# Tail token tiles stored in two halves, and the bias rows of three chunks computed four units sooner, in an attention, layer-norm and feed-forward kernel

## The chip, the cores and the metric

The kernel runs on one core of a Trainium2 chip. The metric is the device time of one launch in microseconds (us). TensorE is called PE in the rows, VectorE DVE, ScalarE ACT, GpSimd POOL, and SyncE SP; SP computes nothing here and issues most of the DMAs, so its rows are those of a queue (SPq).

## What is computed

Attention with a position bias made by a small network, over 4 batches, 8 heads, 576 positions and 64 channels, and behind it a layer norm and a feed-forward block of 512 to 2048 to 512 channels. All inputs are float32.

```python
scores = scale * np.matmul(q, k.transpose(0, 1, 3, 2))
x = (psi_rel / psi_i)[..., None]
h = np.maximum(x @ w1 + b1, 0.0)
bias = h @ w2
scores = scores + bias.transpose(2, 0, 1)[None, :, :, :]
...
xn = (x - mu) / np.sqrt(var + 1e-06) * g_ln
ch = np.maximum(xn @ w_ch1, 0.0) @ w_ch2
return (x + ch).astype(np.float32)
```

The bias depends on the two positions and the head, not on the batch.

## The kernel before

**Units.** The 576 query rows are four chunks of 128 rows (c = 0 to 3) and a tail of 64 rows (c = 4). A unit u is one batch, one chunk and one head (a tail unit holds two heads); there are 144, in the order of the list `ORD`. For a unit, PE forms the scores (`qk`, L391, tile sps), DVE adds the bias and takes the row minimum (`softmax1`, L434), ACT takes the exponential (L438) and a float16 copy (L443, tile e), DVE the float16 rest (L462, L464), SP issues a DMA transpose of that pair (L470, into pt, or into wend for every fifth unit), and PE multiplies with V (`pv`, L480, tile xps). The e tiles are four buffers, and one comes free when its transpose has landed.

**Token tiles.** When the eight heads of 128 tokens are there, the layer norm follows (`ln1`, `ln2`), its result goes through a DMA transpose too (L601, xT), and the feed-forward block runs in steps: 48 matmuls of 128 columns (`ffn_w1`, L709, tile hps, one buffer), the two halves of its ReLU on ACT (L714) and on DVE (L717), and 12 matmuls of 512 columns (`ffn_w2`, L736, tile y). DVE adds y to the tile (L747), and after the last step SP stores it (L751). The 64 tail tokens of two batches share one tile, which is stored by L753. There are 18 tiles, two of them tail tiles.

**Bias rows.** The bias is made in 36 groups of 16 query rows, eight for a chunk. A group is four ReLU instructions (`bias_relu`, one on DVE at L162 and three on ACT at L160), four float32 matmuls, each 32 columns wide, into four quarters of one PSUM tile (`bias_mm`, L181, tile bps; each is two passes, so a whole group reads x8 in the trace and one matmul x2), two ACT copies into a tile ev (L187), and a write of ev to a table in DRAM (L211, nb<-ev). Units read the table back with L326 (ldb<-nb, 128 rows of one head); these reads wait for the chunk's last write. The tiles r, ev, t and u are seven buffers of one pool. Line 922 sets in which unit a group is begun: the eight groups of chunks 1 to 3 are spread over 24 units that end ten units ahead of the chunk's first unit, one group every third unit.

**Order.** The Python code sets the order in which work is offered, and a scheduler that comes with the language merges it into one fixed instruction list for each engine. Each engine goes through its list in order and waits on semaphores.

Of the kernel before, what the change touches and what calls it, by code (L numbers as in the profile page):

```python
# [22 lines left out]
def kernel(  # L23
# [13 lines left out]
    V, S, G, T, SY = nc.vector, nc.scalar, nc.gpsimd, nc.tensor, nc.sync  # L37
# [100 lines left out]
    def after(ins, dep):  # L138
        if dep is not None:
            tc.add_manual_dep(ins.ins, dep.ins.name,  # L140
                              mybir.DependencyInfo(mybir.DependencyClass.Sync,
                                                   mybir.DependencyReason.DATA),
                              reason="pace")
# [73 lines left out]
    for n, (b, c) in enumerate(ORD):  # L217
# [6 lines left out]
    cfirst = {c: min(u for (_, cc), u in ustart.items() if cc == c) for c in range(5)}  # L224
    gorder = [g for c in corder for g in range(8 * c, min(36, 8 * c + 8))]
    gend = {c: sum(len(range(8 * x, min(36, 8 * x + 8))) for x in corder[:corder.index(c) + 1])
            for c in range(5)}
# [178 lines left out]
    def spin(n, last=None):  # L406
        ps = ps_h.tile([128, 512], F32, tag="h", name="spin")
        ones = one_sb.bitcast(BF16)
        for _ in range(n):
            m = T.matmul(out=ps[:, 0:256], lhsT=ones[:, 0:128], rhs=ones, start=True, stop=True)  # L410
            if last is None:
                tc.keep_in_program_order(m)
            else:
                tc.add_manual_dep(m.ins, last.ins.name,
                                  mybir.DependencyInfo(mybir.DependencyClass.NoSync,
                                                       mybir.DependencyReason.DATA),
                                  reason="order")
            last = m
# [3 lines left out]
    def softmax1(u):  # L422
        if not 0 <= u < NU:
            return
        b, c, h = units[u]
        ps = st.pop(u)
        t = ep.tile([128, EW], F32, tag="e", name="t")[:, 0:SEQ]
        m = small.tile([128, 1], F32, tag="m", name="m")
        key = (seg[vis[u]], c, h)
        bias = bt[key]  # L430
        buse[key] -= 1
        if not buse[key]:
            bfree[0] += 1
        ttri[u] = V.tensor_tensor_reduce(out=halves(t), in0=ps[:, :, 0:HS], in1=halves(bias), scale=-0.125,  # L434
                               scalar=3e38, op0=ALU.add, op1=ALU.min, accum_out=m)
        if h == 0:
            l8[b, c] = small.tile([128, NH], F32, tag="l8", name="l8")
        S.activation(t, t, AF.Exp, bias=m, scale=-1.0, accum_out=l8[b, c][:, h:h + 1])  # L438
        if nat_pv(b, c):
            et[u] = (t, None)  # L440
            return
        e16 = e16p.tile([128, 1152], F16, tag="e16", name="e16")
        S.activation(e16[:, 0:SEQ], t, AF.Copy, scale=E_SCALE)  # L443
        et[u] = (t, e16)
# [297 lines left out]
    def ffn_y():  # L742
        while yq:
            k, g, t, y, last = yq.pop(0)
            b, c = tiles[blocks[k][t]]
            x = xt[b, c].rearrange("p a d -> p (a d)")
            V.scalar_tensor_tensor(out=x, in0=y, scalar=ycs[:, g:g + 1], in1=x,  # L747
                                   op0=ALU.mult, op1=ALU.add)
            if last:
                if c < 4:  # L750
                    SY.dma_start(out=out[b, c * 128:c * 128 + 128, :], in_=x)  # L751
                else:
                    SY.dma_start(out=out[b:b + 2, 512:576, :], in_=x)  # L753

    jobs = [(k, qq) for k in range(NBL) for qq in range(4)]
    cur_job = []
# [103 lines left out]
    u = 0  # L860
    while u < NU + 6 or jobs or cur_job or pend or yq:
        if u >= NEARLY:
            ffn_y()
        if u in FILL:
            with tc.high_priority(offset=-600):
                spin(FILL[u], lastpv[0])
        softmax1(u)
        if u == 0:
            for ins in gate:
                after(ins, ttri[0])  # L870
            gate.clear()
            gate_on[0] = False
        ustep[0] = u
        issue_loads(u)
        softmax2(u - 1)
        flush()
        for _ in range(2):
            if wload:
                load_w()
        for _ in range(8):  # L880
            if wdec and 32 - len(wdec) < 2 + (4 * max(0, u - 1) + 2) // 3:
                f, i = wdec.pop(0)
                decode_w(f, i)
                if i == 1 and f + 1 == GROUPS[GOF[f]][1]:
                    w_scale(GOF[f])
        while mm_done[0] < ngroup:
            bias_mm(gorder[mm_done[0]])
            mm_done[0] += 1
        if u % 2:
            first = qk(u + 1)  # L890
            if u >= 27 and first is not None:
                after(first, ttri[max(ttri)])
            qk(u + 2)
        while npv <= u - (LAG if u < 38 else LAG + 1):
            if pv(npv):
                lnq.append([u, len(avail_at) + len(lnq)])
            npv += 1
        for fn in todo.pop(u, []):
            fn()
        for qq in range(4):  # L900
            if wdone[0] >= 8 * qq + 8 and qq not in wready_at:
                wready_at[qq] = u
        if u < NU + 9:
            nav = len([a for a in avail_at if a <= u])
            goal = sum(2 * NF * len(bl) // 4 for bl in blocks if bl[-1] < nav)
            nxt = min((steps_av[bl[-1]] for bl in blocks if bl[-1] >= nav), default=NU + 9)
            mbank += max(0.0, (goal - (ntot - nmicro) - mbank)) / max(1, nxt - u)
            mbank = min(mbank, 2.0)
        else:
            mbank = 1.0  # L910
        flush_lo()
        ffn_y()
        while mbank >= 1.0:
            if not ffn_micro(u):
                break
            mbank -= 1.0
            nmicro -= 1
            if mbank >= 1.0:
                ffn_y()
        bneed = NP + 1 + u if u < 8 else 12  # L920
        for c in (1, 2, 3):
            bneed = max(bneed, gend[c] - 8 + min(8, (u - cfirst[c] + 34) * 8 // 24))
        if u < 28:
            bneed = min(bneed, 12)
        if ngroup < min(36, bneed):
            bias_relu(gorder[ngroup], 1 if u >= 24 else 2)
            ngroup += 1
        for _ in range(2):
            if wspl:
                split_w(*wspl.pop(0))  # L930
        for it in list(lnq):
            if it[0] == u - 1:
                ln1(it[1])
            if it[0] == u - 2:
                ln2(it[1])
                avail_at.append(u + (3 if u < NEARLY else 2))
                lnq.remove(it)
        u += 1
# [53 lines left out]
```

## Time and profile before

| | |
|---|---|
| time, median of 3 runs | 680.51 us (680.23 to 681.94) |
| the profiled execution: time, span | 679.99 us, 678.2 us |
| PE busy | 647.7 us, 96% of the span |
| DVE, ACT, POOL busy | 457.8, 392.0, 97.4 us |
| granted TensorE clock, mean | 0.985 of full speed |

Busy time is the time in which an engine's instructions run. A row of a timeline gives start, duration, engine, line, operation, and in square brackets the idle time before it and what ended that.

### The profile page before, as it was taken

The page shows a single profiled execution, that of the slowest core. Times are in us where ns is not written, and L with a number is a line of the kernel's source. Part 1 is how long each engine was busy: PE and PEld are TensorE (multiplying, and loading weights), DVE is VectorE, ACT ScalarE, POOL GpSimd, SP SyncE. Part 2 cuts the span into 40 slices and gives each one's busy share as a digit, 9 for nine tenths or more (in the row PEclk, how much of TensorE's full clock was granted, in tenths as well). Part 3 has the DMA queues.
Part 4 walks back from the last instruction along what each step waited for, and adds up shares of the span by engine and source line. Part 5 has one row for each costly group of instructions (what it writes and reads, how often), then busy time and mean ns, then how long its engine had stood idle before and what let it go on. Part 6 is the DMA issues. An engine that isn't in the chain of part 4 may idle for free.

```text
span 678.2 us, 19142 instructions
## 1 busy us (share of the span) xinstructions
PE 647.7 (96%) x7929; PEld 448.4 (66%) x7929; DVE 457.8 (68%) x1061; ACT 392.0 (58%) x777; POOL 97.4 (14%) x163
## 2 busy tenths in 40 slices
PE   6889996998999889999899999999999999999997
PEld 4447774676466666666667766666776677677775
DVE  6588999778757567686766575757576676766322
ACT  5565847478957447787764577576554455444110
POOL 5312321011000011111101110111011120000000
PEclk9989997899999999999899999999999999999999
DMA  8999885444659996868869789789996976744100
GB/s 312 294 404 331 307 294 161 143 91 115 143 122 148 223 246 156 173 156 164 172 149 239 134 183 181 136 197 181 201 200 144 166 153 125 121 98 87 33 16 17
DMA packets 186955, 117.24 MB, mean 173 GB/s; under 512 B 163956, under 2 KB 164084, under 8 KB 186868
## 3 DMA queue, kind: packets, MB, share of 16 engines
q1 hardware_dynamic: 177124, 81.00, 55.8%
q0 software_dynamic: 9600, 34.84, 16.6%
q8 instruction: 62, 1.02, 0.6%
q10 hardware_dynamic: 144, 0.18, 0.1%
q14 instruction: 25, 0.20, 0.1%
HBM read 60.51 MB, written 15.63 MB: 112 GB/s over the span
## 4 chain that ended last, share of the span: by engine, by line
PE 50%; DVE 0%; ACT 0%; issue 0%
PE hps L709 19%; PE y L736 18%; PE sps L391 6%; PE xps L480 6%; PE bps L181 1%; DVE v L369 0%; DVE x L747 0%; DVE e L462 0%; ACT e L443 0%; DVE x L516 0%; ACT t L438 0%; DVE e L464 0%
## 5 line engine op out<-in xcount | busy, mean ns | idle before, releaser
L709 PE MATMUL hps<-xT,w 128*128 128x128 f16 x3240 | 196.4, 220 | 5.8 <-DVE hh L717 2.6
L709 PEld LDWEIGHTS <-w 128*128 128x128 f16 x3240 | 184.6, 98 | 11.5 <-issue 5.2
L736 PE MATMUL y<-w,hh 128*128 128x512 f16 x810 | 189.1, 381 | 1.9 <-ACT hh L714 1.8
L438 ACT ACTIVATE t<-t,m 128x576 f32<-128x576 f32 x144 | 111.0, 771 | 132.8 <-DVE m L434 132.2
L736 PEld LDWEIGHTS <-hh 128*128 128x128 f16 x864 | 79.7, 98 | 90.6 <-ACT hh L714 3.3
L462 DVE SCALAR_TENSOR_TENSOR e<-t,e 128x512 f16<-128x512 f32 x120 | 82.8, 690 | 81.8 <-ACT e L443 81.5
L434 DVE CUSTOM_DVE_ANT_0 t<-sps,ldb 128x576 f32<-128x576 f32 x144 | 105.9, 753 | 31.4 <-PE sps L391 21.2
L391 PE MATMUL sps<-kf,qf 64*128 64x288 f32 (+1 forms) x640 | 96.6, 436 | 3.5 <-DVE m L434 3.5
L443 ACT ACTIVATE e<-t 128x576 f16<-128x576 f32 x120 | 80.8, 679 | 9.8 <-DMA pt<-e 3.5
L714 ACT ACTIVATE hh<-hps 128x512 f16<-128x512 f32 x72 | 42.0, 583 | 53.4 <-PE hps L709 47.9
L717 DVE SCALAR_TENSOR_TENSOR hh<-hps,hh 128x512 f16<-128x512 f32 x72 | 49.4, 687 | 34.0 <-ACT hh L714 33.5
L391 PEld LDWEIGHTS sps<-kf,qf 64*128 64x128 f32 (+1 forms) x640 | 48.2, 176 | 35.6 <-issue 17.5
L480 PEld LDWEIGHTS <-pt 128*128 128x128 f16 (+1 forms) x1456 | 49.3, 100 | 30.5 <-issue 24.9
L747 DVE SCALAR_TENSOR_TENSOR x<-y,ycs,x 128x512 f32<-128x512 f32 x58 | 43.4, 748 | 32.2 <-PE y L736 32.0
L480 PE MATMUL xps<-v,pt 128*128 128x64 f16 (+1 forms) x1456 | 59.0, 195 | 1.9 <-DMA pt<-e 1.1
L291 POOL DMA_DIRECT2D kf<-in_k_s_dram x56 | 31.1, 556 | 161.4 <-PE sps L391 114.3
L304 POOL DMA_DIRECT2D qf<-in_q_main_dram x32 | 18.5, 577 | 162.4 <-PE xps L480 82.6
L187 ACT ACTIVATE ev<-bps,cb_sb,par_sb 128x144 f32<-128x144 f32 (+27 forms) x48 | 26.0, 593 | 26.2 <-PE bps L181 26.0
L160 ACT ACTIVATE r<-psi_sb,par_sb 128x448 f32<-128x448 f32 (+23 forms) x72 | 39.7, 614 | 0.0
L569 POOL TENSOR_SCALAR rs<-mv 128x1 f32<-128x1 f32 x18 | 9.9, 549 | 146.3 <-DVE mv L568 138.3
L438 ACT ACTIVATION_READ_ACCUMULATOR t<-t,m 128x1 f32 x144 | 27.0, 188 | 0.0
L181 PE MATMUL bps<-r,nw_sb 128*32 128x448 f32 (+24 forms) x200 | 26.9, 494 | 0.0
(121 smaller groups left out, 641.4 us busy)
## 6 DMA issues: line engine op xcount, KB each, us to landing
kf<-in_k_s_dram POOLq DMA_DIRECT2D x56, 288.0 KB, 4.8
w<-in_w_ch_dram SPq DMA_DIRECT2D x22, 512.0 KB, 8.7
ldb<-nb SPq DMA_DIRECT2D x32, 288.0 KB, 4.5
qf<-in_q_main_dram POOLq DMA_DIRECT2D x32, 256.0 KB, 4.6
nb<-ev SPq DMA_DIRECT2D x24, 296.0 KB, 3.4
vf<-in_v_p_dram POOLq DMA_DIRECT2D x16, 320.0 KB, 7.5
out_dram<-x SPq DMA_DIRECT2D x18, 256.0 KB, 2.1
wend<-in_w_ch_dram SPq DMA_DIRECT2D x8, 512.0 KB, 4.8
```

What stands on the lines that cost most here:

```text
L160: S.activation(r[:, 0:n], psi_sb[:, 0:n], AF.Relu, bias=pr_sb[:, g4:g4 + 1], scale=1.0)
L391: m = T.matmul(out=o, lhsT=l, rhs=kk, start=True, stop=True, tile_position=(64 * hf, 64 * e))
L434: ttri[u] = V.tensor_tensor_reduce(out=halves(t), in0=ps[:, :, 0:HS], in1=halves(bias), scale=-0.125, scalar=3e38, op0=ALU.add, op1=ALU.mi ...
L438: S.activation(t, t, AF.Exp, bias=m, scale=-1.0, accum_out=l8[b, c][:, h:h + 1])
L443: S.activation(e16[:, 0:SEQ], t, AF.Copy, scale=E_SCALE)
L462: V.scalar_tensor_tensor(out=e16[:, 640:1152], in0=t[:, 0:512], scalar=E_SCALE, in1=e16[:, 0:512], op0=ALU.mult, op1=ALU.subtract)
L480: T.matmul(out=o, lhsT=p[:, m], rhs=v[:, j, a, :], start=(i == 0), stop=(i == len(ops) - 1))
L709: T.matmul(out=h[:, idx * n:idx * n + n], lhsT=w[:, wo + kk * 128:wo + kk * 128 + 128], rhs=xT[k][:, xo + kk, 0:n], start=(i == 0), stop=( ...
L714: S.activation(hh[:, 0], h, AF.Relu)
L717: V.scalar_tensor_tensor(out=hh[:, 1], in0=h, scalar=0.0, in1=hh[:, 0], op0=ALU.max, op1=ALU.subtract)
L736: T.matmul(out=yps[k][t], lhsT=hh[:, a, o:o + 128], rhs=w[:, wo:wo + 512], start=(f == f0 and i == 0), stop=(f == f1 - 1 and i == 2))
L747: V.scalar_tensor_tensor(out=x, in0=y, scalar=ycs[:, g:g + 1], in1=x, op0=ALU.mult, op1=ALU.add)
```

## The change

Two edits. The store of a tail tile, one DMA with a 2 x 64 x 512 pattern in DRAM, becomes two DMAs of 64 x 512 each. And the number 34 in the rule that begins the groups becomes 38, so that each group of chunks 2 and 3 is begun four units sooner. For chunk 1 other limits in the same rule bind (nothing of it before unit 28, one group a unit): only its last two groups move, from units 35 and 38 to 34 and 35.

```diff
-                    SY.dma_start(out=out[b:b + 2, 512:576, :], in_=x)
+                    for e in range(2):
+                        SY.dma_start(out=out[b + e, 512:576, :], in_=x[64 * e:64 * e + 64])
...
         for c in (1, 2, 3):
-            bneed = max(bneed, gend[c] - 8 + min(8, (u - cfirst[c] + 34) * 8 // 24))
+            bneed = max(bneed, gend[c] - 8 + min(8, (u - cfirst[c] + 38) * 8 // 24))
```

The first edit changes no other row in any engine's list. The second reorders PE, DVE, ACT and SP from the 352-column group of chunk 1 on. POOL's list stays as it is.

PE, the last two groups of chunk 1 (352 and 336 columns). Before, the four matmuls of a group stand together, the first group behind a step of the feed-forward block:

```order
L709 LDWEIGHTS wend
L709 MATMUL hps<-xT,wend 128x128
L181 MATMUL bps<-r,nw_sb 32x352 x4
L480 LDWEIGHTS pt
L480 MATMUL xps<-v,pt 128x64
```

and the second ahead of a pair of tail scores:

```order
L736 MATMUL y_2974<-wend,hh 128x512
L181 MATMUL bps<-r,nw_sb 32x336 x4
L391 MATMUL sps<-kf,qf 64x288 x8
L480 LDWEIGHTS wend
L480 MATMUL xps<-v,wend 128x64
```

With the change the first group is four single matmuls; one stands seven feed-forward matmuls ahead of this piece, and the other three are these:

```order
L181 MATMUL bps<-r,nw_sb 32x352
L391 MATMUL sps<-kf,qf 128x288 x4
L181 MATMUL bps<-r,nw_sb 32x352
L709 LDWEIGHTS wend
L709 MATMUL hps<-xT,wend 128x128
L181 MATMUL bps<-r,nw_sb 32x352
```

The second group, a feed-forward step sooner than before, is in three pieces among matmuls of the V product; the third, a single matmul too, stands three V matmuls behind this piece:

```order
L480 MATMUL xps<-v,pt 128x64
L181 MATMUL bps<-r,nw_sb 32x336 x2
L480 LDWEIGHTS pt
L480 MATMUL xps<-v,pt 128x64
L181 MATMUL bps<-r,nw_sb 32x336
L480 LDWEIGHTS pt
L480 MATMUL xps<-v,pt 128x64
```

Each of the sixteen later groups stands in PE's list with its four matmuls together, before and with the change.

SP, around the store of the first tail tile. Before (numbers behind e_ and x_ tell tiles apart):

```order
L211 DMA nb_125<-ev 16x8x592
L470 DMA_TRANSPOSE pt<-e_2822 128x9x128
L753 DMA out_dram<-x 2x64x512
L601 DMA_TRANSPOSE xT<-x_2872 128x8x128
L470 DMA_TRANSPOSE pt<-e_2880 128x9x128
L470 DMA_TRANSPOSE pt<-e_2965 128x9x128
L470 DMA_TRANSPOSE pt<-e_3001 128x9x128
L751 DMA out_dram<-x 128x512
L211 DMA nb_125<-ev 16x8x592
L326 DMA ldb<-nb_125 128x576 x3
L470 DMA_TRANSPOSE wend<-e_3098 128x9x128
```

and with the change, from the same write on:

```order
L211 DMA nb_125<-ev 16x8x592
L754 DMA out_dram<-x 64x512 x2
L211 DMA nb_125<-ev 16x8x592
L470 DMA_TRANSPOSE pt<-e_2839 128x9x128
L601 DMA_TRANSPOSE xT<-x_2889 128x8x128
L470 DMA_TRANSPOSE pt<-e_2898 128x9x128
L326 DMA ldb<-nb_125 128x576 x5
L751 DMA out_dram<-x 128x512
L470 DMA_TRANSPOSE pt<-e_2983 128x9x128
L470 DMA_TRANSPOSE pt<-e_3011 128x9x128
```

The chunk's last write of bias rows has moved ahead of five DMAs, four of them transposes, and five table reads follow three transposes later instead of three right behind the write.

PE, near the second tail store, at the step of the feed-forward block that uses weights w_129 to w_132. Before, its 48 L709 matmuls are followed by one unit's scores, nine V matmuls (the last is shown) and a bias group, and then at once by the first of its own L736 matmuls:

```order
L480 LDWEIGHTS pt
L480 MATMUL xps<-v,pt 128x64
L181 MATMUL bps<-r,nw_sb 32x369 x4
L736 LDWEIGHTS hh
L736 MATMUL y_5215<-w_129,hh 128x512
```

With the change the 48 matmuls of the next step (w_133 to w_136) stand ahead of them:

```order
L709 LDWEIGHTS w_136
L709 MATMUL hps<-xT,w_136 128x128
L736 LDWEIGHTS hh
L736 MATMUL y_5234<-w_129,hh 128x512
L736 LDWEIGHTS hh
```

A whole L709 step now lies between the matmuls that fill hps and those that read the hh made from it.

## Rows read from the trace of the kernel before

**Rows 1.** The page, its head and part 1: span, busy time (share of span).

```profile
span 678.2 us, 19142 instructions
PE 647.7 (96%) x7929; PEld 448.4 (66%) x7929; DVE 457.8 (68%) x1061; ACT 392.0 (58%) x777; POOL 97.4 (14%) x163
```

**Rows 2.** Busy time by stretch: stretch, its length, engines, granted clock, DMA share, GB/s.

```profile
200.00:260.00 60.00, 56.46 (x821) 38.91 (x819) 38.38 (x92) 34.69 (x71) 6.81 (x12) 1.00 0.97 190
...
326.00:340.00 14.00, 12.00 (x171) 9.72 (x170) 11.47 (x23) 9.81 (x18) 2.11 (x3) 0.88 0.86 174
340.00:672.00 332.00, 332.00 (x4228) 234.34 (x4227) 201.29 (x458) 165.47 (x324) 35.02 (x57) 1.00 0.69 140
```

**Rows 3.** Waits of PE, 200 to 260 us: total us, times, longest.

```profile
PE hps L709 <- DVE hh L717: 2.6, 2, 1.3
PE xps L480 <- DMA wend<-e: 0.5, 1, 0.5
PE xps L480 <- DVE x L543: 0.4, 1, 0.4
```

**Rows 4.** DMA, 208 to 220 us: 40 slices, busy tenths and GB/s; one issue's landing.

```profile
DMA  8899999939617538994999866111111199999997
GB/s 111 213 367 236 266 258 213 175 27 75 61 55 178 185 142 236 251 142 105 94 82 51 53 22 42 55 48 48 48 48 55 38 181 281 288 191 293 432 493 307
...
xT<-x SPq DMA_TRANSPOSE x1, 9.6
```

**Rows 5.** DMA, 327 to 338 us: GB/s in 40 slices.

```profile
GB/s 402 321 177 144 243 195 40 128 286 211 30 0 30 37 52 45 45 52 54 97 128 179 228 227 342 201 197 143 74 74 48 48 48 52 55 271 284 283 217 263
```

**Rows 6.** The sixteen ordinary stores of 128 rows (L751): issue to landing.

```profile
DMA to landing us min/median/max: 2.0/2.1/4.8
```

**Rows 7.** DMA issues, 193 to 198 us: count, KB each, median us to landing.

```profile
ldb<-nb SPq DMA_DIRECT2D x2, 144.0 KB, 3.3
pt<-e SPq DMA_TRANSPOSE x1, 3.2
```

**Rows 8.** Timeline of SP's queue: start, us to issue, line.

```profile
207.06 1.31 SPq L470 DMA_TRANSPOSE pt<-e  x1
208.46 0.83 SPq L753 DMA_DIRECT2D out_dram<-x  x1
209.39 5.07 SPq L601 DMA_TRANSPOSE xT<-x  x1
...
223.53 0.58 SPq L211 DMA_DIRECT2D nb<-ev  x1
228.76 1.28 SPq L326 DMA_DIRECT2D ldb<-nb  x3
```

**Rows 9.** Timeline of ACT and PE, 223 to 225.5 us.

```profile
223.21 0.68 ACT L443 ACTIVATE e<-t 128x576 f16<-128x576 f32 x1 [2.71 <-DMA pt<-e]
...
223.80 0.58 ACT L714 ACTIVATE hh<-hps 128x512 f16<-128x512 f32 x1
...
225.41 2.84 PE L709 MATMUL hps<-xT,w 128*128 128x128 f16 x48 [1.28 <-DVE hh L717]
```

**Rows 10.** Timeline of PE, 196 to 204.5 us: bias matmuls and what follows them.

```profile
196.47 0.81 PE L181 MATMUL bps<-r,nw_sb 128*32 128x368 f32 x2
197.21 1.25 PE L736 MATMUL y<-w,hh 128*128 128x512 f16 x5
...
203.60 0.80 PE L181 MATMUL bps<-r,nw_sb 128*32 128x352 f32 x8
204.33 0.58 PE L480 MATMUL xps<-v,pt 128*128 128x64 f16 x14
```

**Rows 11.** Timeline of DVE, ACT and PE, 329 to 334 us.

```profile
329.41 0.76 DVE L434 CUSTOM_DVE_ANT_0 t<-sps,ldb 128x576 f32<-128x576 f32 x1 [1.29 <-DMA nb<-ev]
...
332.48 0.58 ACT L714 ACTIVATE hh<-hps 128x512 f16<-128x512 f32 x1
...
333.11 0.61 PE L736 MATMUL y<-w,hh 128*128 128x512 f16 x2 [1.57 <-ACT hh L714]
```

## The prediction

> **What bounds the kernel now.** First the page's busy times: PE is busy for 647.7 of 678.2 us, and no other engine for more than 68% [rows 1]. A share over the whole span says little, so next comes the busy time by stretch. From 340 to 672 us PE is busy in every microsecond at full clock [rows 2]: nothing that the change takes from another engine or from DMA can shorten that stretch, and a change there can only hurt. What can be won lies where PE stands still behind the first moved instruction, at about 201 us: 60 - 56.46 = 3.54 us between 200 and 260, and 14 - 12.00 = 2.00 us between 326 and 340 [rows 2]. In the second stretch the granted clock also averages 0.88, that is, part of it ran at the lower level, 1.2 GHz, directly after PE had stood; (1 - 0.88) x 14 = 1.7 us. So 7.2 us is the most that can come back. Then the list of PE's waits says what ended those gaps: of the 3.5 us, 2.6 are two waits for hh (1.3 each), 0.5 a transpose, 0.4 a DVE result [rows 3]. In the second stretch 1.57 us are again a wait for hh [rows 11].
>
> **The tail store.** Before, it is one DMA issued at 208.46 [rows 8]. In the DMA view of that stretch the strip falls to one tenth and 38 to 55 GB/s for seven slices of 0.3 us in a row, and the same 48 GB/s returns behind the second tail store [rows 4, 5]. One tenth of 16 engines is about two. 256 KB at 48 GB/s take 5.5 us, where the ordinary stores of the same size land in a median of 2.1 us, issue and all [rows 6]. I read it as a DMA that runs on two engines, one for each value of its outer dimension. What makes this matter stands behind it in SP's list: the transpose xT takes 5.07 us to issue, where the transpose ahead of the store took 1.31, and 9.6 us to land [rows 8, 4]. The others follow late. Their e buffers come free late, so ACT, which works in order, stands 2.71 us ahead of an L443 at 223.21 and only then reaches the L714 that PE needs; L717 follows, and PE has stood for 1.28 us [rows 9].
>
> Do two stores of 64 x 512 each use all engines? The trace has no such store. The nearest rows are the two loads of 64 rows, 144 KB each, which land in 3.3 us [rows 7]; at two engines' 48 GB/s each alone would need 3.1 us and the pair 6. Ordinary stores give 2.1. I take the ordinary behaviour. Two issues instead of one cost SP at least nothing and at most another 0.83 us [rows 8]; the in-order queue behind them has just won about 4 us (5.07 less 1.31), so they cost nothing.
>
> The Trainium skill, DMA: Bandwidth & Descriptors, Why a DMA increments its semaphore by 16 and not by 1, states how many engines a DMA takes: the largest number up to 16 that divides the slowest dimension of both sides, so 2 for the old store and 16 for either new one. The trace agrees on the old one with its 48 GB/s; no run so far shows the new one.
>
> Term: the wait at 225.41 goes, **-1.28 us**. Bounds: 0 (if the transposes are late for another reason too) and -1.28.
>
> **The split groups.** The part that costs stands in PE's list. The last two groups of chunk 1 were four matmuls together and become four single ones, and a pair with two singles. In the trace the 352-column group together holds PE from 203.60 to 204.33, 0.73 us. A single matmul of the 368-column group holds it from 196.47 to 197.21, 0.74 us [rows 10]. So the four quarters run side by side, and one quarter alone costs as much as all four; a pair must then cost that much too. Then the first group costs 4 x 0.73 instead of 0.73, and the second 3 x 0.73 instead of 0.73: 5 x 0.73 = **+3.6 us** of PE. Nothing hides it where PE is the bound. It would be hidden only as far as PE would have stood anyway soon behind it: bounds 0 and +3.6. I take it whole, since I count those waits as gone.
>
> A rule of the skill would make it dearer still: TensorEngine Tiling (Array Packing), Key Properties, says that changing the tiling mode drains TensorE, and each single matmul adds two such changes. The trace shows no price for it, 0.74 us for a single matmul against 0.73 for a group; by the row the sum stays at +3.6, by the rule it would be larger by an amount that the page doesn't give.
>
> **The rest of the first stretch.** Behind the wait at 225.41, PE stands 2.26 us more by 260 (1.3 + 0.5 + 0.4). In SP's list the chunk's last row write goes out at 223.53, and the table reads behind it at 228.76 [rows 8]; transposes stand behind those. With the change that write comes ahead of four transposes, and five reads stand together behind three of them. The write's new place is directly behind the store, which goes out at 208.46 now; with the store's 0.83 us and the split's 3.6 us it goes out near 213, ten us earlier, so the reads find it landed, and the later transposes no longer share the DMA engines with as many of them. Against that, the first group of chunk 2 now falls into the same 250 us. I take half: **-1.1 us**, bounds 0 and -2.26.
>
> **The second stretch.** At 329.41 DVE's L434 has waited 1.29 us for a write of bias rows to release a buffer of the common pool; ACT's L714 slips to 332.48, and PE waits 1.57 us with its L736 [rows 11]. PE could not fill the time, since before the change that L736 comes almost directly behind the L709 matmuls it depends on. Two things move it: groups begun four units sooner put another group's write there, and in the new list a whole L709 step lies between. That step is 2.84 us long [rows 9], more than the 1.57 us of the wait. So the 2.00 us and the 1.7 us of clock go: **-3.7 us**, bounds 0 and -3.7.
>
> **What costs nothing.** The sixteen other moved groups keep their four matmuls together; their ACT, DVE and DMA work is the same and lies beside a PE that is busy in all of 340 to 672 us [rows 2]. Their writes pass transposes in SP's list by one or two places each, 0.6 us of issue [rows 8]. If that cover goes, a late transpose stops PE for about what the known waits were, 0.4 to 1.3 us.
>
> **Sum.** -1.28 + 3.6 - 1.1 - 3.7 = -2.5 us against the profiled execution's 679.99: 677.5. That execution lies 0.5 us under the median of the three runs, 680.51, so against the median it is **678.0 us**, 0.37% less. With all waits gone it is 3.6 less, 676.9; nothing in the trace allows more, apart from the spread of the runs.
>
> **Rivals.**
> *The gain is eaten.* The store does what it should, but one new wait appears. The nearest candidate is SP's row write of the 336-column group, which now stands ahead of a transpose and waits for ACT's L187, which waits for the last single matmul, up to 3.6 us later than without the split. PE, ACT and DVE behind that transpose then stand. The price lies between the known waits, 0.4 us [rows 3] and 2.71 us [rows 9], say 1 to 2: 679.0 to 680.0, within 0.3% of before. For it: SP's list is in order, and DMA is 0.97 busy there [rows 2]. Against: the transposes are no longer held up by the store, which took more from them than the split does.
> *Slower: the writes of bias rows are the cause, not the store.* Only the wait at 225.41 goes, and the other two remain, because a row write holds a pool buffer or SP's list wherever it is put. Then -1.28 + 3.6 = +2.3 us, 682.8. It decides as soon as less than 1.6 us of the 7.2 comes back. For it: the wait at 329.41 names the write, not the store. Against: PE's new order covers that place.
> *The halves use few engines as well.* Then the store does as before, -1.28 falls away, and the rest stands: 679.3. Against: the 64-row loads.
> *The cost of the split is hidden.* If the waits of the first stretch are set by DMA alone and stay where they are in time, the 3.6 us fall into them and nothing is lost or won there; only the second stretch is won: 680.5 - 3.7 = 676.8.
>
> **Chances.** 0.3% is 2.0 us, about what a measurement of this kernel can tell from no change; with the split's 3.6 us, 5.6 of the 7.2 us must come back for faster, and the forecast has 6.1, near that border. The forecast with its neighbours (5.6 us and more, 0.44; split hidden, 0.08) 0.52; eaten 0.24 and few engines 0.10, together 0.34; slower 0.14. So faster 0.52, same 0.34, slower 0.14. The likeliest case alone spans 676.9 to 678.5. The range for 8 in 10 goes from 676.4, under that floor by the 0.5 us by which executions differ, up into the slower case, to 681.8.
>
> **What would show it.** Right: no stretch of one-tenth DMA behind the tail stores, the xT transpose behind the first issued in about 1.3 us, no wait for hh near 225; seven separate holds of 0.7 us for the two groups; PE without a gap, at full clock, from 320 to 340. Wrong: 48 GB/s still there; single matmuls that cost less than 0.7 us each; PE busy time up by 3.6 us with gaps that stay; a clock below 1.00 anywhere behind 200 us.

## The result, and the profile after

| | before | changed |
|---|---|---|
| median of 6 runs each, us | 680.66 (679.91 to 685.05) | 689.02 (687.20 to 693.01) |
| ratio, 95% interval | | 1.0111 (1.0085 to 1.0138) |
| profiled execution: time, span, us | 679.99, 678.2 | 693.01, 691.2 |
| granted TensorE clock, mean | 0.985 | 0.978 |

The changed kernel is 8.4 us slower. The forecast was 678.0 us, and the range ended at 681.8. The profiled execution is the longest of the six, so sizes are taken from the medians and places from the trace. In the experiments below, eight executions that lie over 1.5% above the fastest of their kernel, four of them above 1000 us, are left out of medians and ratios. Head and part 1 of the page of after (columns as in [rows 1]):

```profile
span 691.2 us, 19138 instructions
PE 654.9 (95%) x7929; PEld 452.5 (65%) x7929; DVE 457.6 (66%) x1061; ACT 390.8 (57%) x777; POOL 95.4 (14%) x163
```

PE is busy 7.2 us longer than in [rows 1] with the same 7929 matmuls; DVE and ACT do what they did. The busy time by stretch of after (stretch, length, engines, clock, DMA share, GB/s) tells where the rest is:

```profile
200.00:260.00 60.00, 55.60 (x675) 35.87 (x675) 33.55 (x80) 32.22 (x66) 5.13 (x9) 0.94 0.86 177
260.00:340.00 80.00, 78.48 (x1076) 54.74 (x1071) 54.65 (x132) 58.58 (x122) 10.39 (x19) 1.00 0.80 163
340.00:400.00 60.00, 56.88 (x704) 39.49 (x704) 40.53 (x93) 34.14 (x68) 5.80 (x10) 0.97 0.86 168
...
326.00:340.00 14.00, 14.00 (x196) 10.14 (x193) 8.58 (x24) 10.21 (x21) 1.60 (x3) 1.00 0.86 164
```

In the stretch from 326 to 340 us, where PE stood for 2.00 us at a clock of 0.88 [rows 2], PE is busy throughout and at full clock. But from 200 to 260 PE now stands 4.4 us, with the clock at 0.94; it stands 1.5 us between 260 and 340, and 3.1 us between 340 and 400, at 0.97, where it never stood before [rows 2]. Standing and half clock (the latter (1 - 0.94) x 60 + (1 - 0.97) x 60 = 5.4 us) are 14.4 us here, against 5.5 + 1.7 = 7.2 us behind 200 us before. Add 3.5 us for the split (below): 10.7 of the 13.0 us by which the spans differ. The first bias matmul starts at 156.0 us instead of 153.3, after a part in which the lists are the same: that is variation between executions, and covers the rest.

PE's waits in after, 200 to 400 us (total us, times, longest):

```profile
PE hps L709 <- DVE hh L717: 6.3, 3, 3.1
PE xps L480 <- DMA pt<-e: 2.7, 2, 2.4
```

The wait for hh of [rows 3] is still the first, longer and later. The longest one, in the timeline of after, 345 to 362 us:

```profile
345.10 1.49 SPq L754 DMA_DIRECT2D out_dram<-x  x2
...
346.69 0.56 SPq L211 DMA_DIRECT2D nb<-ev  x1
...
347.87 0.22 DVE L464 SCALAR_TENSOR_TENSOR e<-t,e 128x64 f16<-128x64 f32 x1
...
349.19 0.22 DVE L464 SCALAR_TENSOR_TENSOR e<-t,e 128x64 f16<-128x64 f32 x1
...
351.52 0.35 SPq L326 DMA_DIRECT2D ldb<-nb  x1
...
351.99 4.83 SPq L470 DMA_TRANSPOSE pt<-e  x2
...
359.30 0.68 ACT L443 ACTIVATE e<-t 128x576 f16<-128x576 f32 x1 [4.05 <-DMA pt<-e]
...
359.88 0.58 ACT L714 ACTIVATE hh<-hps 128x512 f16<-128x512 f32 x1
...
360.75 0.68 DVE L717 SCALAR_TENSOR_TENSOR hh<-hps,hh 128x512 f16<-128x512 f32 x1
...
361.49 0.80 PE L709 MATMUL hps<-xT,w 128*128 128x128 f16 x6 [3.12 <-DVE hh L717]
```

Read it from the bottom. PE waits 3.12 us for hh; hh is late because ACT's L714 stands behind an L443 that waited 4.05 us for an e buffer; the buffer is held by a transpose that SP issued only at 351.99. Above it stands the reason: the chunk's last row write was issued at 346.69, the first table read of chunk 2 directly behind it, and that read has to wait until the write has landed. The DMA view of 344 to 360 us has the write's landing, 4.8 us after its issue, that is at 351.5:

```profile
nb<-ev SPq DMA_DIRECT2D x1, 296.0 KB, 4.8
```

SP goes through its list in order, so from 347.25 to 351.52 it issues nothing, although the two e tiles for the next transposes had been finished at 348.1 and 349.4 (the two L464). The list of the queue's own waits gives 4.2 us to this read, ended by the DMA nb<-ev. The Trainium skill, Perfetto Trace Analysis, Per-instruction lifecycle: what the profiler-reported window actually captures, says that an instruction's wait for a semaphore lies outside the time recorded for it. The trace agrees: the read has 0.35 us, and in the timeline the 4.3 us are only to be seen as a hole between two rows. No transpose is issued from 345.0 to 352.0, 7 us.

SP's list of before holds the same write and read; here is its timeline, 336 to 362 us:

```profile
346.86 1.87 SPq L470 DMA_TRANSPOSE wend<-e  x1
348.89 1.29 SPq L470 DMA_TRANSPOSE pt<-e  x1
350.69 0.53 SPq L211 DMA_DIRECT2D nb<-ev  x1
353.73 1.29 SPq L326 DMA_DIRECT2D ldb<-nb  x3
355.19 3.57 SPq L470 DMA_TRANSPOSE pt<-e  x2
```

There the read waited 2.5 us, two transposes had just gone out, and 5.0 us passed without one: PE did not wait. With the change the write stands directly behind the two halves of the tail store, and ahead of transposes that are ready. It is the place that counts, not the length of the wait: over its whole span the queue of before waits 10.5 us for row writes ahead of table reads, in four waits of up to 4.6 us, and that of after 6.7 us, in two of up to 4.2.

The other place, SP's queue in after, 204 to 250 us:

```profile
213.25 1.16 SPq L754 DMA_DIRECT2D out_dram<-x  x2
216.26 0.55 SPq L211 DMA_DIRECT2D nb<-ev  x1
...
218.44 1.78 SPq L601 DMA_TRANSPOSE xT<-x  x1
...
221.91 2.87 SPq L326 DMA_DIRECT2D ldb<-nb  x5
224.87 0.43 SPq L751 DMA_DIRECT2D out_dram<-x  x1
225.48 7.21 SPq L470 DMA_TRANSPOSE pt<-e  x2
...
234.65 9.37 SPq L470 DMA_TRANSPOSE pt<-e  x3
```

and ACT and PE there (timeline of 232 to 243 us):

```profile
240.46 0.58 PE L480 MATMUL xps<-v,pt 128*128 128x64 f16 x14 [2.38 <-DMA pt<-e]
240.50 0.68 ACT L443 ACTIVATE e<-t 128x576 f16<-128x576 f32 x1 [5.24 <-DMA pt<-e]
...
242.70 0.58 PE L709 MATMUL hps<-xT,w 128*128 128x128 f16 x4 [1.65 <-DVE hh L717]
```

The reads find their write landed, as the prediction said. But five of them, 288 KB each, go out together, the transposes behind them take 7.21 us for two and 9.37 us for three to issue, and PE stands 2.38 and then 1.65 us. From 220 to 246 us the transposes into pt and wend take a median of 8.3 us from issue to landing, the longest 11.7; in before these are 5.5 and 6.7.

The DMA view of after, 212 to 226 us (count, KB each, median us to landing), for the store:

```profile
out_dram<-x SPq DMA_DIRECT2D x2, 128.0 KB, 2.3
...
xT<-x SPq DMA_TRANSPOSE x1, 5.1
```

The halves land in 2.3 us, near the ordinary stores' 2.1 [rows 6], and the xT behind them in 5.1 us instead of 9.6 [rows 4]. The second pair of halves, at 345.10, takes 5.0 us to land. And PE's list, 204 to 215 us, for the split:

```profile
204.37 0.78 PE L181 MATMUL bps<-r,nw_sb 128*32 128x352 f32 x2
205.09 0.56 PE L709 MATMUL hps<-xT,wend 128*128 128x128 f16 x7
...
212.66 0.76 PE L181 MATMUL bps<-r,nw_sb 128*32 128x336 f32 x4
213.35 0.20 PE L480 MATMUL xps<-v,pt 128*128 128x64 f16 x1
```

A single matmul holds PE for 0.72 us, a pair for 0.69; the seven pieces hold it for 4.9 us where two groups held it for 1.4, so the split costs 3.5 us.

### The profile page after: what moved, and what is told of

Its sections match the earlier page's. It is cut to its first block, busy times and chain, and to the rows that moved or that the text cites. A ratio compares the mean times of both kernels' runs of the same rounds, so it can differ in the third digit from the quotient of the medians.

```text
span 691.2 us, 19138 instructions
## 1 busy us (share of the span) xinstructions
PE 654.9 (95%) x7929; PEld 452.5 (65%) x7929; DVE 457.6 (66%) x1061; ACT 390.8 (57%) x777; POOL 95.4 (14%) x163
## 4 chain that ended last, share of the span: by engine, by line
PE 46%; DMA 2%; ACT 2%; DVE 1%; issue 0%; SPq 0%; DVEq 0%; ACTq 0%
PE hps L709 17%; PE y L736 17%; PE sps L391 6%; PE xps L480 5%; DMA nb<-ev 1%; PE bps L181 1%; DMA pt<-e 1%; ACT e L443 0%; ACT v L366 0%; ACT t L438 0%; ACT ev L187 0%; DVE e L462 0%; ACT r L160 0%; DVE v L369 0%; DVE t L434 0%
## 5 line engine op out<-in xcount | busy, mean ns | idle before, releaser
L709 PE MATMUL hps<-xT,w 128*128 128x128 f16 x3240 | 199.8, 222 | 9.5 <-DVE hh L717 6.3
L709 PEld LDWEIGHTS <-w 128*128 128x128 f16 x3240 | 187.7, 99 | 15.7 <-issue 9.5
L736 PE MATMUL y<-w,hh 128*128 128x512 f16 x810 | 189.4, 381 | 0.4 <-ACT hh L714 0.3
L736 PEld LDWEIGHTS <-hh 128*128 128x128 f16 x864 | 79.9, 98 | 88.8 <-issue 2.7
L434 DVE CUSTOM_DVE_ANT_0 t<-sps,ldb 128x576 f32<-128x576 f32 x144 | 105.8, 753 | 28.6 <-PE sps L391 17.3
L443 ACT ACTIVATE e<-t 128x576 f16<-128x576 f32 x120 | 80.8, 679 | 13.3 <-DMA pt<-e 10.9
L714 ACT ACTIVATE hh<-hps 128x512 f16<-128x512 f32 x72 | 42.1, 584 | 55.0 <-PE hps L709 49.5
L181 PE MATMUL bps<-r,nw_sb 128*32 128x448 f32 (+24 forms) x200 | 30.7, 494 | 0.0
L569 POOL TENSOR_SCALAR rs<-mv 128x1 f32<-128x1 f32 x18 | 8.2, 457 | 148.3 <-DVE mv L568 148.3
```

The lines of the kernel that those rows point to most:

```text
L709: T.matmul(out=h[:, idx * n:idx * n + n], lhsT=w[:, wo + kk * 128:wo + kk * 128 + 128], rhs=xT[k][:, xo + kk, 0:n], start=(i == 0), stop=( ...
L714: S.activation(hh[:, 0], h, AF.Relu)
L736: T.matmul(out=yps[k][t], lhsT=hh[:, a, o:o + 128], rhs=w[:, wo:wo + 512], start=(f == f0 and i == 0), stop=(f == f1 - 1 and i == 2))
```

## The experiments

Ratios are to the kernel before on the same chip, with 95% intervals; its medians were 682.19, 682.09, 681.58 and 682.51 us in the four series below. They are not quotients of the medians listed here, which differ from them by up to 0.24%. Where runs of different series are compared, it is by their ratios.

| run | median, us | ratio |
|---|---|---|
| store halves alone | 682.77 | 1.0012 (0.9983 to 1.0040) |
| groups sooner alone | 691.07 | 1.0137 (1.0101 to 1.0172) |
| store halves, chunks 2 and 3 sooner | 686.37 | 1.0085 (1.0055 to 1.0115) |
| store halves, chunk 1 sooner | 688.77 | 1.0075 (1.0043 to 1.0108) |
| changed, two groups joined | 690.33 | 1.0110 (1.0057 to 1.0164) |
| changed, reads held back | 681.84 | 0.9987 (0.9958 to 1.0017) |
| changed, reads held back for chunks 2 and 3 | 685.73 | 1.0047 (1.0027 to 1.0067) |
| changed, 5 e and 8 read buffers | 682.93 | 1.0018 (0.9983 to 1.0054) |
| changed, 8 read buffers | 683.50 | 1.0022 (0.9993 to 1.0052) |
| changed, 5 e buffers | 683.85 | 1.0020 (0.9995 to 1.0045) |
| changed, reads held back, two groups joined | 678.21 | 0.9947 (0.9920 to 0.9974) |
| before with store halves, all groups joined | 678.83 | 0.9944 (0.9912 to 0.9975) |
| before, 5 e and 8 read buffers | 683.40 | 1.0021 (0.9992 to 1.0050) |
| the same with store halves, all groups joined | 679.96 | 0.9982 (0.9947 to 1.0017) |
| changed, all remedies, all groups joined | 677.43 | 0.9926 (0.9895 to 0.9957) |

### First series: which edit

*The store halves alone*, on the kernel before:

```diff
-                    SY.dma_start(out=out[b:b + 2, 512:576, :], in_=x)
+                    for e in range(2):
+                        SY.dma_start(out=out[b + e, 512:576, :], in_=x[64 * e:64 * e + 64])
```

> Only the tail store in two halves; every engine's list is otherwise that of the kernel before. Theory A (the time is lost by the bias groups: 3.6 us of PE for the split matmuls, the rest by transposes that land late): 676.5 to 679.5 us, the wait of 1.28 us near 225 gone, no stretch at 48 GB/s. Theory B (the halves themselves cost: what they let through collides with the loads and transposes behind): 683 us or more, with a new wait of PE behind 208 or 328 us.

1.0012: no difference. The wait at 225 us is gone from its trace; waits of 1.4 us near 333 and of 3.3 us near 450 stand in it. The store costs nothing that the run can tell, and its 1.28 us don't show either. In this trace a read near 226 us waits 6.8 us for its row write, and PE's waits from 200 to 260 us come to 1.9 us: a long hole in the queue need not cost much.

*The groups sooner alone*, on the kernel before, with its one store:

```diff
-            bneed = max(bneed, gend[c] - 8 + min(8, (u - cfirst[c] + 34) * 8 // 24))
+            bneed = max(bneed, gend[c] - 8 + min(8, (u - cfirst[c] + 38) * 8 // 24))
```

> Only the groups sooner, the tail store one DMA as before. Theory A: 687 to 693 us, at least as slow as both edits together, since the slow store comes on top. Theory B: 680 to 685 us, the split's 3.6 us less what it hides.

1.0137: this edit carries the loss. In SP's queue the write goes out at 340.11, behind the one store, and lands at 350.65; the first read behind it goes out at 350.67, and PE stands 4.6 us. Behind the two halves the same write took 4.8 us to land.

*Chunks 2 and 3 alone, and chunk 1 alone*, both with the new store:

```diff
-            bneed = max(bneed, gend[c] - 8 + min(8, (u - cfirst[c] + 38) * 8 // 24))
+            bneed = max(bneed, gend[c] - 8 + min(8, (u - cfirst[c] + (38 if c > 1 else 34)) * 8 // 24))
```

(for chunk 1 alone, `c == 1`.)

> Store in halves; groups of chunks 2 and 3 four units sooner, those of chunk 1 as before, so the groups of 352 and 336 columns keep their four matmuls together. Theory A: no split cost, and the table reads of chunk 1 three at a time as before: 3.6 us of PE and the waits of 4.0 us near 240 (with 3.4 us of lower clock) go, 678 to 682 us. Theory B: 685 us or more.

> Store in halves; only the last two groups of chunk 1 sooner. Theory A: the split's 3.6 us and the waits near 240 stay, 684 to 688 us. If instead the sixteen groups of chunks 2 and 3 cost most: 678 to 682 us.

Both are slower, by 0.85% and 0.75%. The first has no additional split, so the split can't be the whole cause, as the first theory had it. SP's queue in that run, 336 to 362 us, has the pattern of after again, and PE stands 3.7 us behind it:

```profile
338.72 0.56 SPq L211 DMA_DIRECT2D nb<-ev  x1
343.42 0.34 SPq L326 DMA_DIRECT2D ldb<-nb  x1
343.88 4.71 SPq L470 DMA_TRANSPOSE pt<-e  x2
```

Not all the loss of the run of chunks 2 and 3 need lie there: its trace has another wait of PE, 3.5 us near 255 us for a DVE result (x, L543; 0.4 us in before). It stands far ahead of that hole in SP's queue, and its cause is open.

The profiled execution of the chunk-1 run (682.86 us) is the shortest of that run and shows only 3.6 us of waits; its trace explains nothing of its median. Together the two parts come to 1.6%, the whole change to 1.1%: if anything, the parts do not add up.

### Second series: the chain

*The two groups joined.* In the changed kernel the first three matmuls of both groups also wait for the group's last ReLU (`rl4`):

```diff
-                    T.matmul(out=flat[32 * s:32 * s + 32, a:b], lhsT=nw2_sb, rhs=rs[s][:, a:b],
-                             start=True, stop=True)
+                    mm = T.matmul(out=flat[32 * s:32 * s + 32, a:b], lhsT=nw2_sb, rhs=rs[s][:, a:b],
+                                  start=True, stop=True)
+                    if s < 3 and gi in (14, 15):
+                        after(mm, rl4)
```

> The changed kernel, but the first three matmuls of the 352-column and the 336-column group also wait for the group's last ReLU, so that the four stand together again; the writes and reads of the table stand about where the change put them. Theory S (the split is a real cost of PE, 3.5 us in the profiles): each of the two groups holds PE for about 0.73 us, PE's busy time falls by some 3.5 us and the kernel is 2 to 4 us faster than the changed kernel, that is still 2 to 5 us slower than before, since the waits behind the reads stay. Rival (the split falls into time in which PE would stand anyway): same as the changed kernel, 6 to 9 us slower than before.

1.0110, as the changed kernel, though the interval is wide. PE's waits in its trace, 200 to 400 us:

```profile
PE xps L482 <- DMA pt<-e: 5.3, 1, 5.3
PE hps L711 <- DVE hh L719: 4.8, 2, 3.8
```

10.1 us against 9.0 in after: in these two executions PE gets to the same waits sooner and stands longer. The run's interval leaves room for the whole 3.5 us all the same.

*The same in the kernel before, for all groups of L181, with the store halves* (the condition is only `s < 3`; before, five groups stand in twelve pieces). These are the 24 groups of chunks 1 to 3; the other twelve of the 36 are made at L201 and stay as they are:

> The kernel before with its groups where they were, the tail stores in two halves, and in every group the first three matmuls wait for the last ReLU, so that all 36 groups hold PE once (before, the 432-, 416-, 400-, 384- and 368-column groups stand in two or three pieces, seven pieces more than five). Theory S: seven pieces of 0.73 us less, some 5 us of PE busy time, and the kernel is 3 to 5 us faster than before (0.993 to 0.996). Rival (PE waits at these places for something else and the saved time turns into a wait): same as before, 0.998 to 1.002.

0.9944, 3.8 us faster. PE's busy time falls from 647.7 to 641.9 us, about the 5.1 us of seven pieces.

*Five e buffers and eight buffers of table reads*:

```diff
-    KB, LB = 8, 9
+    KB, LB = 8, 8
...
-    e16p = ctx.enter_context(tc.tile_pool(name="e16", bufs=4))
+    e16p = ctx.enter_context(tc.tile_pool(name="e16", bufs=5))
```

> The changed kernel with five buffers for the tile e instead of four, so that a late transpose stops ACT one unit later (buffers of the table reads fall from nine to eight to make room). Theory E (a late transpose stops ACT for want of an e buffer, and through it PE): the waits of ACT's L443 and of PE for hh near 240, 295 and 358 us shrink, and the kernel is 3 to 8 us faster than the changed kernel. Rival (PE waits for the transposes themselves at its V product, whatever buffers ACT has): same as the changed kernel, within 0.3%.

1.0018: the loss is gone. But with eight buffers the reads also stand later in SP's list, which the expectation had overlooked; the fourth series takes the two apart.

*The table reads held back*, each until the newest L434 offered ahead of it is done:

```diff
-                    SY.dma_start(out=raw, in_=nbias[c][:, h, :])
+                    ld = SY.dma_start(out=raw, in_=nbias[c][:, h, :])
+                    if c > 0:
+                        after(ld, ttri[max(ttri)])
```

> The changed kernel, but each table read L326 of chunks 1 to 3 also waits for the current unit's L434, so that it stands some transposes later in SP's list and not directly behind the chunk's last row write; lists of PE, ACT and DVE are unchanged. Theory H (a read that waits in SP's in-order list for the write to land holds back the ready transposes behind it): the 4.3 us wait of SP ahead of the first read of chunk 2 goes, PE's 3.1 us wait near 358 us and its half-clock stretch with it, and that near 240 us shrinks: 3 to 8 us faster than the changed kernel. Rival (the waits come from the reads' traffic on the DMA engines, wherever the reads stand in the list): same as the changed kernel, within 0.3%.

0.9987: the whole loss is gone, 8.5 us by the ratios, with the groups and the split where the change put them. In the trace PE, ACT, DVE and POOL have the same instructions in the same order as in after; only SP's list differs. SP's queue in this run, 338 to 366 us:

```profile
337.40 1.57 SPq L756 DMA_DIRECT2D out_dram<-x  x2
339.06 1.16 SPq L211 DMA_DIRECT2D nb<-ev  x1
340.53 3.01 SPq L472 DMA_TRANSPOSE pt<-e  x2
344.65 1.23 SPq L603 DMA_TRANSPOSE xT<-x  x1
...
352.07 0.57 SPq L326 DMA_DIRECT2D ldb<-nb  x1
```

Store and write are followed at once by the transposes, and the read comes when the write has landed. Busy time by stretch in this run:

```profile
200.00:260.00 60.00, 60.00 (x794) 38.65 (x796) 39.04 (x94) 36.15 (x74) 5.71 (x10) 1.00 0.90 184
260.00:340.00 80.00, 78.63 (x1053) 54.42 (x1046) 56.35 (x132) 61.30 (x126) 10.39 (x19) 1.00 0.84 167
340.00:400.00 60.00, 60.00 (x782) 41.93 (x777) 41.09 (x98) 35.41 (x70) 7.75 (x14) 1.00 0.91 195
```

PE is busy and at full clock from 200 to 260 and from 340 to 400 us. In the latter DMA moves 195 GB/s instead of 168: in after the DMA engines had room. A wait of 1.3 us for hh near 288 us stays; before has none between 260 and 300 us.

### Third series: do the parts add up

*Both remedies for the changed kernel: reads held back, two groups joined*, the diffs of the second series together.

> The changed kernel with both edits of the last two runs on it: the 352- and 336-column groups of chunk 1 kept together, and the table reads held back by the unit's L434. Keeping the groups together alone gave nothing beside the waits. Theory S2 (the split costs PE 3.5 us, but the end is set by late transposes where those waits stand; with the waits gone the 3.5 us show): 3 to 4 us faster than the run with the reads held back alone, 677.5 to 679 where before takes 682. Rival (the saved PE time turns into waits again): within 0.2% of the run with the reads held back, 681 to 683.

0.9947, against 0.9987 with the reads held back alone: 2.7 us, and PE's busy time falls from 648.6 to 644.1 us. Each group is one hold again (PE's timeline, 195 to 212 us):

```profile
204.61 0.80 PE L181 MATMUL bps<-r,nw_sb 128*32 128x352 f32 x8
208.90 0.77 PE L181 MATMUL bps<-r,nw_sb 128*32 128x336 f32 x8
```

So the split has its price once the transposes are in time, though the intervals of the two runs just overlap.

*All remedies and all groups of L181 joined, on the changed kernel*: the three diffs of the second series together, with `s < 3` as the only condition.

> The changed kernel with all three edits: all 36 groups kept together (twelve pieces of 0.73 us fewer than in the changed kernel, 8.8 us of PE), the table reads held back, and five e buffers with eight buffers of table reads. If the pieces cost PE their full price wherever it doesn't wait: 672 to 675 (8.8 us less than about 682, some of it lost to waits before 200 us, where keeping groups together left PE waiting 3.4 us longer). If each saving turns into a new wait: 678 to 682.

0.9926, the lowest ratio of the study; its interval overlaps those of the two runs at 0.994 to 0.995. Its groups stand in twelve pieces fewer than in the changed kernel, 8.8 us of PE; part of that is lost again ahead of 200 us, where a joined group waits 1.9 us for ACT's ReLU: between 155 and 200 us PE waits 5.2 us in this trace and 2.6 in that of the run above.

*The kernel before with five e buffers and eight read buffers, and that with store halves and all groups joined*, by the same diffs.

> The kernel before with five e buffers instead of four and eight buffers of table reads instead of nine, nothing else. Theory E2 (what a fifth buffer gives back in the changed kernel are the waits that the moved groups made; before has only the waits at 225, 240 and 331 us, some 4 us, of which those for hh behind a late transpose, 2.6 us, go): 1 to 4 us faster than before. Rival (four buffers cost the kernel several us wherever the groups stand, and the change adds little of its own): 6 us faster or more.

> The kernel before with its groups at their places, tail stores in halves, all groups kept together, and five e buffers with eight buffers of table reads. If the fifth buffer and the joined groups add up: 2 to 4 us faster than the joined groups alone, 674 to 677 where before takes 682. If the fifth buffer gives nothing where the groups weren't moved: the same as the joined groups alone, 678 to 680.

1.0021 and 0.9982: these buffers give nothing to the kernel before that the runs can tell. Both theories of the first run missed: they expected at least 1 us. Waits of PE near 242 us (2.0), 337 us (2.3) and 457 us (1.9) stand in its trace. What the buffers cure in the changed kernel is the change's own damage. The second run does not look as fast as the joined groups without the buffers (0.9944), but the two intervals overlap; its runs spread from 675.9 to 685.9 us.

### Fourth series: buffer or order, and which place

*Eight read buffers alone, and five e buffers alone*, both on the changed kernel. The first has only the `LB` line of the diff above; the second, with SP's list as in after:

```diff
-    e16p = ctx.enter_context(tc.tile_pool(name="e16", bufs=4))
+    e16p = ctx.enter_context(tc.tile_pool(name="e16", bufs=5))
...
-    xtp = ctx.enter_context(tc.tile_pool(name="xt", bufs=4))
+    xtp = ctx.enter_context(tc.tile_pool(name="xt", bufs=3))
```

> The changed kernel with eight buffers of table reads instead of nine, and still four e buffers. The first read of chunk 2 no longer stands directly behind the chunk's last row write, but behind five transposes. Theory H (the place of the reads in SP's list): 5 to 8 us faster than the changed kernel, 681 to 684 where before takes 682. Theory E (the fifth e buffer did it): same as the changed kernel, 688 to 690.

> The changed kernel with five e buffers instead of four, nine buffers of table reads as before, and three buffers of xT instead of four to make room; SP's list is that of the changed kernel, the lists of PE, ACT and DVE differ only ahead of 200 us. Theory H (only the place of the reads matters; a transpose held back is late for PE's V product as well): same as the changed kernel within 0.4%, 686 to 691. Theory E (ACT stands for want of an e buffer, PE behind it): 5 to 8 us faster, 681 to 684.

1.0022 and 1.0020: each alone takes nearly all the loss away. Neither theory is right alone; they fit as two links of one chain. With five e buffers SP still stands, as the queue's timeline shows (340 to 364 us):

```profile
343.83 1.19 SPq L754 DMA_DIRECT2D out_dram<-x  x2
345.13 0.56 SPq L211 DMA_DIRECT2D nb<-ev  x1
350.64 0.34 SPq L326 DMA_DIRECT2D ldb<-nb  x1
351.09 4.06 SPq L470 DMA_TRANSPOSE pt<-e  x2
```

The hole is 5.0 us, longer than in after, yet from 340 to 400 us PE never stands: the fifth buffer bridges it. The first place isn't safe with it; in the profiled execution, the longest of this run, the one wait of PE behind 200 us is there, 6.2 us for a transpose.

*Reads held back for chunks 2 and 3 only*:

```diff
-                    SY.dma_start(out=raw, in_=nbias[c][:, h, :])
+                    ld = SY.dma_start(out=raw, in_=nbias[c][:, h, :])
+                    if c > 1:
+                        after(ld, ttri[max(ttri)])
```

> The changed kernel with the table reads held back for chunks 2 and 3 only; five reads of chunk 1 stand together near 222 us, as the change put them. If the wait of the first read of chunk 2 near 351 us carries the loss: 4 to 7 us faster than the changed kernel, 682 to 685. If the reads of chunk 1 near 222 us carry it: 1 to 3 us faster, 686 to 688, with the waits near 240 us still there.

1.0047. PE's wait for hh at 361 us in after is gone from the trace, and the waits near 236 to 244 and at 296 us are there. About half the loss (0.64%, 4.4 us) hangs on the reads of chunks 2 and 3, the other half (0.60%, 4.1 us) on those of chunk 1.

## Why the prediction was wrong

**The step that failed** is what the moved row writes and table reads do to SP's list, and the prediction had it wrong in two terms. For chunks 2 and 3, "What costs nothing" counted what the moved writes take to issue ("one or two places each, 0.6 us of issue") and left out what stands behind a write: the first table read of a chunk, which waits in the same list until the write has landed, and then the transposes behind that read. The move put the pair directly behind the tail store and ahead of ready transposes near 346 us; the runs price this at 4.4 us. For chunk 1, "The rest of the first stretch" saw the five reads together and the write landed, took this for a gain of 1.1 us, and bounded it at 0: that the transposes behind the reads could land later than before was no case of it. The runs price these reads at 4.1 us. Together it is 8.5 us (from the changed kernel to the reads held back). The prediction's fallback, a late transpose at 0.4 to 1.3 us each, was too small: there were four waits of 1.5 to 3.1 us, and behind both places part of the time ran at the lower clock, 1.2 GHz (mean clock 0.83 from 240 to 260 us, 0.96 from 360 to 400), a price that the prediction had put on the wait of before and not on a new one. Its own view held the warning: [rows 8] show the write at 223.53 and the read behind it at 228.76, a 4.7 us hole in the queue, which was read as the reads' place and not as SP's standing still.

**The split**, +3.6 us: right in PE's list (3.5), and 2.7 us by the ratios once the transposes are in time. In the changed kernel itself the joined groups gained nothing that the run can tell. On the rule of the Trainium skill that each change of tiling mode drains TensorE (TensorEngine Tiling (Array Packing), Key Properties) the prediction misread its rows: a whole group stands between full-array matmuls too, so its 0.73 us [rows 10] hold the same two changes as the 0.72 us of a single matmul. What the changes cost, if anything, is in both numbers and in the sum already; these rows can't price it, and the rule gave no reason to expect more.

**The store**, -1.28 us: the mechanism is right. The halves land in 2.3 us, and the xT behind them is issued in 1.78 us instead of 5.07 [rows 8] (2.08 with the store halves alone). That agrees with the rule on the number of engines, which the prediction quoted from the Trainium skill's page DMA: Bandwidth & Descriptors. The gain itself does not show (1.0012); the interval reaches from -1.2 to +2.7 us, with -1.28 just outside. The wait at 225 goes, and other waits stand elsewhere.

**The two waits**, -1.1 and -3.7 us: the waits themselves went. PE has no gap from 320 to 340 us in after, and with the reads held back none from 200 to 260 us either. In size they are too large together with the store: the run with both remedies has everything but the split's cost, where these terms promise -6.1 us, and gets -3.6 (-5.5 to -1.8 by its interval). Its trace still has 4.6 us of waits behind 200 us, at other places (2.1 near 230, 1.2 near 285, 1.3 near 430). The forecast's own state, the split paid and the waits gone, is the run with the reads held back: it measured -0.13% (-0.42 to +0.17), where the forecast's -0.37% is still inside.

**As a sum** of ratios: -3.6 for the waits, +2.7 for the split, +8.5 for the transposes held back make +7.6 us, which is the 1.11% of the changed kernel. The three are steps from one run to the next, so they must add up; this is no separate test.

**The rivals.** The slower one had the right sign and nearly the right object ("a row write holds ... SP's list wherever it is put"), but priced it as waits that stay (+2.3) and not as new ones. "The gain is eaten" had the right pattern, a row write ahead of transposes, with ACT and PE behind; it looked at the write's wait for ACT instead of the read's wait for the write, and had 1 to 2 us for it. The chance of slower, 0.14, was too low: PE's cover of 332 us without a gap was taken as safety, though a place where PE never waits is also one where any new wait is a whole loss.

**What stays open:** whether the five reads near 222 us hurt by their place in the list or by their traffic. Four instead of five were enough to remove the waits in one profiled execution, and holding them back was too. Open too is what makes the wait near 288 to 296 us, which holding the reads back leaves, and the one near 255 us in the run of chunks 2 and 3.

## What to carry to other kernels

When an edit moves a DMA in an in-order queue, look for the instruction that waits for it to land and for what stands behind that one: what can be lost is the landing time, taken from everything ready behind it, and in the timeline a hole between two rows of the queue is its only sign (the list of the queue's waits names it). A hole with nothing ready behind it costs little: before has longer ones. Ask how many buffers the late one's producer still has, since one more buffer hides the same hole. And a saving of busy time on the bounding engine is worth its price only where that engine is not already waiting: here the same joined groups gave 2.7 us with the transposes in time, and nothing that one run could tell (within some 4 us) while they were late.

## What the runs showed of the hardware

A 32-column matmul alone holds PE as long as four side by side (0.72 against 0.73 us), so pieces of a group that a scheduler has spread cost PE some 0.7 us each; joining them, together with the store halves, made the kernel before 0.56% faster. DMA transposes that SP elsewhere issues in 1.3 us [rows 8] took 3.6 us each (7.21 for two) where five table reads of 288 KB had just gone out. The reads are not the whole reason: with the reads held back, the same two took 5.44 us directly behind a store of 256 KB. And executions of one kernel differ by more than most effects here: the 25 to 35 runs of before in each series lie between 678.1 and 691.4 us, but for one of 1613.7, so that one profile shows where waits can be, and only the medians of a dozen runs what they cost.
